# Odd keys moved by SyncE in two parts, key tiles in another order, more unread products, GpSimd pieces of 480 columns

## The chip, the cores and the metric

The kernel runs on one core of a Trainium2 chip. The core has TensorE (matrix products, "PE" in the profile; its weight loads are "PEld"), VectorE ("DVE"), ScalarE ("ACT"), GpSimd ("POOL") and SyncE ("SP"), which here only issues DMAs. Each works through its own list of instructions in order, and semaphores hold an instruction until what it needs is there. The metric is the device time of one execution in microseconds; six executions of the kernel before give a median of 742.34 us (739.19 to 746.28).

## The reference: what is computed

Two branches over the same input x (2048 rows of 512) are mixed by a gate.

```python
q = x @ wq          # 32 heads of 16
k, v = x @ wk, x @ wv        # one key and one value head for all
a = softmax(q k^T / 4) v  @ wo
z = gelu(x @ w_in);  z1, z2 = halves of 688;  z2 = layernorm(z2)
b = (z1 * (w_sp @ z2 + b_sp)) @ w_out
g = sigmoid((x * gate_w).sum(-1));  out = g * a + (1 - g) * b
```

Attention is the bulk: 32 heads times 2048 queries times 2048 keys, so 134 million exponentials.

## The kernel before

**Units and blocks.** A unit is four heads of the same parity with 512 queries; there are 32 units. A unit has 64 blocks: 16 key tiles of 128 keys (kt = 0 to 15) times four groups g of one head each. A block is one score product on TensorE with 32 rows of weights (`s_mm`, recorded on line L313): keys from `KA`, queries from `QA`, 512 columns of PSUM out. `KA` has two planes. In plane 0 the keys stand in rows 32g to 32g+15, and they serve the even units; in plane 1 they stand in rows 32g+16 to 32g+31, for the odd units.

**Two ways to the exponential.** Two blocks at a time (1024 columns) go to ScalarE, whose exponential (`exp_op`, L631) writes them to `P`. Four blocks of one key tile are a batch for VectorE instead: `d_A` (L655) turns 1024 columns of PSUM into a linear term in `X`, twice for each batch, and `d_square` (L667) squares all 2048 columns twice; what comes out approximates the exponential, up to a correction by the products with `MC` and `CC`. Of the second squaring, pieces of `GE` = 416 columns go to GpSimd (`g_piece`, L674): none, one or two for each batch, and VectorE squares the 2048, 1632 or 1216 columns that are left. A piece is made to wait for the VectorE instruction ahead of a `d_A`, so that it runs beside that `d_A`. Products with the values (`ps<-P,V` and `ps<-X,V`) add the blocks up over the keys in one bank; when a unit is complete, VectorE transposes the sum (L685), GpSimd forms the reciprocal and scales (L691, L694, L697), and VectorE transposes back to `OT` (L700).

**The order of keys.** `KL` lists the key tiles. Within a unit ScalarE takes blocks from the front of that list, VectorE's batches from its back.

**Making K.** x arrives in four chunks of 512 rows, transposed by DMA. Chunk c gives key tiles 4c to 4c+3: four products (`k_mm`) and a copy from PSUM to plane 0 by VectorE (`k_ev`, L355). When all four chunks are there, `k_shift` (L359) has GpSimd issue four DMAs of 64 KB that copy plane 0 to plane 1. In `gate_and_k` and `g_MC` the correction is made from the last seven tiles of `KL`; `Kt` (L429) holds two of each chunk's four key tiles, repeated for eight heads.

**The other branch.** SyncE loads x, w_in, b_sp, w_o and w_out, and then `ld_wT(0)` (L302), four transposing loads of w_sp's first quarter, each of which waits for the one before. The products with w_in are spread between the score products; when all of z2 is there, ScalarE does all GELUs in one stretch, and TensorE computes z1 meanwhile. The products with w_sp, w_out and w_o fill the gaps after that.

**What sets the order.** A planner in the kernel's Python code writes the order of every engine's list before the program is built. It keeps a clock for TensorE, ScalarE and VectorE, gives each candidate a ready time, a cost and a priority, and always takes the next for the engine that is free first. Costs are constants: 917 ns for an exponential, 1134 for a `d_A`, `GNS` for a GpSimd piece (a fixed part and a part for each column), with `GLAT` ahead. `T["K1"]` is the time from which it lets odd units be used. Score products for ScalarE come first, and no other TensorE work is placed that would end after the next of them is due. `keep_pick` puts in unread products: it adds up the work of the last 3.4 us, counting a full 512-column product as one, and where the sum is under `KEEP` it offers a product of zeros that nothing reads, or of ones into a free bank; under `LOW` with a better priority.

Of the kernel before, what the change touches and what calls it, by code (L numbers as in the profile page):

```python
# [15 lines left out]
S = 2048  # L16
D = 512
DH = 16
# [13 lines left out]
ZMAX = 25.0  # L32


KL = (0, 1, 2, 4, 5, 8, 9, 12, 13, 6, 10, 14, 15, 11, 7, 3)

NPB = 21
NX = 6
# [2 lines left out]
NMAX = 7  # L41
# [8 lines left out]
DMARG = 50.0  # L50
DRAW = 115.0
RIDE = 0.0
GE = 416
GLAT = 160.0
GNS = (60.0, 2.0)
EMARG = 50.0
EXPT = (0, 491, 917, 1343)
SLATE = 535.0
FREE = 60.0
SEEN = 204.0  # L60
KEEP = 7.5
LOW = 6.5
MMARG = 120.0
PMARG = 200.0
PRE = 12
# [107 lines left out]
def build_kernel(nc, x_d, wq_d, wk_d, wv_d, wo_d, win_d, wsp_d, bsp_d, wout_d, gw_d, out_d):  # L173
    es = ExitStack()
    with es:
# [24 lines left out]
        KA = sb("KA", [128, 2, S], B16)  # L200
        QA = sb("QA", [128, NQ, 512], B16)
        V1 = sb("V1", [128, NKT, 32], B16)
        KT0 = sb("KT0", [128, NKT, DH], B16)
        Kt = sb("Kt", [128, 8, 128], B16)
# [68 lines left out]
        def dma(eng, fn, r=(), w=(), n=16, tag="", after=()):  # L273
            return op(eng, fn, r=r, w=w, dma=n, tag=tag, after=after)
# [23 lines left out]
        def ld_wT(tc):  # L298
            prev = []
            for k in range(4):  # L300
                r0 = 512 * tc + 128 * k
                prev = [dma("sp", lambda q, r0=r0, k=k: q.dma_start_transpose(wT[:, :, 128 * k:128 * k + 128], wsp_d[r0:r0 + 128, :]),  # L302
                            w=[("wT", k)], tag="wT", after=prev)]
        ld_wT(0)

        for g in range(4):
            op("dve", lambda v, g=g: v.tensor_scalar(wk_rep[:, :, 32 * g:32 * g + 16], wk_sb[:], 0.25, None, ALU.mult), r=["wk"], w=["wk_rep"])
# [38 lines left out]
        def setT(k):  # L346
            def f(t):
                T[k] = t
            return f
# [4 lines left out]
        def k_ev(c, b):  # L354
            op("dve", lambda v: v.tensor_copy(KA[:, 0, 512 * c:512 * c + 512], bank(b)), r=[bkey(b)], w=[("K", 0, c)], tag="Kev")  # L355

        def k_shift():
            for g in range(4):
                dma("pool", lambda q, g=g: q.dma_start(KA[32 * g + 16:32 * g + 32, 1, :], KA[32 * g:32 * g + 16, 0, :]),  # L359
                    r=[("K", 0, c) for c in range(4)] + ["KA1"], w=[("K", 1, g)], tag="Ksh")  # L360

        def g_K(c):
            def done(t):
                T[("K", 0, c)] = t
                if c == 3:
                    k_shift()
                    T["K1"] = t + 4500
            return Group("K%d" % c, [(C512, lambda dt=dt: k_mm(c, dt, BM)) for dt in range(4)], [(600, lambda: k_ev(c, BM))],
                         lambda: when(("x", c)), done)

# [46 lines left out]
        def g_V(c):  # L417
            def piece(k, dt):
                t0 = 512 * c + 128 * k
                return lambda: mm(bank(BM, 33, 64 * k), xT[:, dt, t0:t0 + 128], wvg[:, dt, 0:33], dt == 0, dt == 3,  # L420
                                  ["wv", "gw", "wvk", ("x", c)], [BMK], tag="V")
            src = bank(BM, 256).rearrange("p (k w) -> p k w", w=64)
            e1 = lambda: op("dve", lambda v: v.tensor_copy(V1[:, 4 * c:4 * c + 4, 0:DH], src[:, :, 0:DH]), r=[BMK], w=[("V", c)], tag="Vev")
            e2 = lambda: op("dve", lambda v: v.tensor_copy(gs[:, 4 * c:4 * c + 4].unsqueeze(2), src[:, :, 32:33]), r=[BMK], w=[("gs", c)], tag="gsev")
            e3 = lambda: op("dve", lambda v: v.tensor_copy(KT0[:, 4 * c:4 * c + 4, :], src[:, :, 16:32]), r=[BMK], w=[("KT0", c)], tag="ktev")

            def done(t):
                T[("V", c)] = t
                dve_q.append((330, lambda: op("dve", lambda v: v.tensor_copy(  # L429
                    Kt[:, 2 * c:2 * c + 2, :].rearrange("p k (h d) -> p k h d", d=DH),  # L430
                    KT0[:, 4 * c + 2:4 * c + 4, :].unsqueeze(2).broadcast_to([128, 2, 8, DH])), r=[("KT0", c)], w=[("Kt", c)], tag="Kt"), t, setT(("Kt", c))))
                if c == 3:
                    gate_and_k()
            def all_():
                for k in range(4):
                    for dt in range(4):
                        piece(k, dt)()
            return Group("V%d" % c, [(480, all_)], [(150, e1), (100, e2), (130, e3)],
                         lambda: when(("x", c), "wvg"), done)
# [15 lines left out]
        def g_MC():  # L455
            pieces = []
            for h in range(2):
                for i in range(NMAX):
                    kt = KL[15 - i]
                    pieces.append((90, lambda h=h, i=i, kt=kt: mm(  # L460
                        bank(BM, 32 * (NMAX - i), 256 * h + 32 * i).rearrange("p (n e) -> p n e", e=32),
                        Kt[:, 2 * (kt // 4) + kt % 2, :] if h == 0 else ones[:, 0:128], V1[:, kt, :].unsqueeze(1).broadcast_to([128, NMAX - i, 32]),
                        i == 0, i == NMAX - 1, [("Kt", kt // 4), ("V", kt // 4), "ones"], [BMK], tag="MC")))
            msrc = bank(BM, 32 * NMAX).rearrange("p (n e) -> p n e", e=32).unsqueeze(2).broadcast_to([128, NMAX, 8, 32])
            mk = mke[:].unsqueeze(1).unsqueeze(3).broadcast_to([128, NMAX, 8, 32])
            e1 = lambda: op("dve", lambda v: v.tensor_tensor(MC[:], msrc, mk, ALU.mult), r=[BMK, "mke"], w=["MC"], tag="MC")  # L466
            e2 = lambda: op("dve", lambda v: v.tensor_scalar(ct[:, 0, :], bank(BM, 32 * NMAX, 256), E0, None, ALU.mult), r=[BMK], w=["ct0"], tag="CC")
            cc = CC[:, :, :].rearrange("p n e -> p (n e)")
            e3 = lambda: op("dve", lambda v: v.tensor_copy(cc, ct[:, 0, :]), r=["ct0"], w=["CC"], tag="CC")
            e4 = lambda: op("dve", lambda v: v.tensor_tensor(ct[:, 1, :], ct[:, 0, :], cc, ALU.subtract), r=["ct0", "CC"], w=["ct1"], tag="CC")  # L470
            e5 = lambda: op("dve", lambda v: v.tensor_scalar(ct[:, 1, :], ct[:, 1, :], s01[:, 1:2], None, ALU.mult), r=["ct1", "s01"], w=["ct1"], tag="CC")
            e6 = lambda: op("dve", lambda v: v.scalar_tensor_tensor(cc, cc, s01[:, 0:1], ct[:, 1, :], ALU.mult, ALU.add), r=["CC", "ct1", "s01"], w=["CC"], tag="CC")
            def some(h):
                for c_, f_ in pieces[NMAX * h:NMAX * h + NMAX]:
                    f_()
            return Group("MC", [(500, lambda: some(0)), (500, lambda: some(1))], [(1950, e1), (320, e2), (320, e3), (320, e4), (250, e5), (320, e6)],
                         lambda: when(*[(k, c) for k in ("Kt", "V") for c in range(4)]), setT("MC"))
# [140 lines left out]
        def s_mm(b, blk):  # L618
            u, kt, g = blk
            par = u % 2  # L620
            rk = [("K", 0, kt // 4)] if par == 0 else [("K", 1, g)]
            mm(bank(b), KA[32 * g:32 * g + 32, par, 128 * kt:128 * kt + 128], QA[32 * g:32 * g + 32, (u // 2) % NQ, :], True, True,
               rk + [("Q", (u // 2) % NQ)], [bkey(b)], tp=(32 * g, 0), tag="S")

# [870 lines left out]
```

## Time and profile before

| | |
|---|---|
| six runs | 739.19 to 746.28 us, median 742.34 |
| the profiled execution | 739.42 us, its span 737.6 us |
| busy, of the span | PE 94%, DVE 97%, ACT 97%, POOL 41% |
| exponentials on ScalarE | 752, the first at 9.17 us, the last ends at 726.8 us |
| GELU stretch on ScalarE | 164.3 to 189.0 us |
| granted TensorE clock, mean | 0.998 of full speed |

The span is the time from the first to the last instruction of the profiled execution. A group line names the source line, the engine, the operation and the tiles, then how often it ran, its busy time and the mean length of one; the idle time at its end is that of the engine just before these instructions, with what ended it. A record can overlap the next one on the same engine, so the mean length can be more than the step from one to the next. "PEclk" is the granted clock in tenths for 40 slices of the span, where 9 is 90% or more. A timeline line has the start and the length in us, the engine (a "q" marks its issuing part), the line and the operation.

### The profile page before, as it was taken

The numbers are of one execution on the slowest core, as the hardware profiler recorded it, in microseconds if no ns is written. First come the engines' busy times: TensorE is split into PE (matmuls) and PEld (weight loads), VectorE is DVE, ScalarE is ACT, GpSimd is POOL, SyncE is SP. The second block draws the span as 40 slices with busy tenths as digits, with TensorE's granted clock in tenths as the row PEclk, the third lists the DMA queues.
The fourth block names the chain that finished last, engine by engine and source line by source line (L and its number), as shares of the span: only waits on it lengthen the run. The fifth ranks groups of instructions, "written<-read, shape, count | busy, mean of one in ns | idle before, by whom it ended". The sixth has DMA issues, their size and how long they took to land.

```text
span 737.6 us, 14117 instructions
## 1 busy us (share of the span) xinstructions
PE 692.3 (94%) x5529; PEld 191.6 (26%) x5529; DVE 713.2 (97%) x821; ACT 717.8 (97%) x781; POOL 303.0 (41%) x304
## 2 busy tenths in 40 slices
PE   8899989989899999999999999999999999999995
PEld 2322222223222222222222322222222222222221
DVE  7999999999999999999999999999999999999996
ACT  5999999999999999999999999999999999999994
POOL 4245444340444344444344443444554433334440
PEclk9999999999999999999999999999999999999999
DMA  9810000000000001400000140000004000000001
GB/s 202 190 30 1 1 1 1 2 1 0 1 1 1 2 1 30 94 15 8 1 1 1 31 94 16 8 1 1 1 21 96 16 15 1 1 1 1 1 1 33
DMA packets 49115, 17.06 MB, mean 23 GB/s; under 512 B 44146, under 2 KB 48978, under 8 KB 49043
## 3 DMA queue, kind: packets, MB, share of 16 engines
q1 hardware_dynamic: 45986, 15.02, 9.0%
q10 hardware_dynamic: 2928, 0.82, 0.6%
q8 instruction: 45, 0.74, 0.4%
q0 software_dynamic: 128, 0.26, 0.2%
q14 instruction: 28, 0.22, 0.1%
HBM read 3.25 MB, written 2.10 MB: 7 GB/s over the span
## 4 chain that ended last, share of the span: by engine, by line
ACT 58%; PE 19%; issue 18%; DVE 3%; POOL 1%; ACTq 0%; POOLq 0%
ACT P L631 56%; PE ps L313 13%; PE ps L312 6%; DVE X L655 1%; ACT z L521 1%; DVE X L667 1%; ACT z L529 1%; DVE MC L466 0%; POOL bspz L264 0%; POOL KA L261 0%; DVE KA L355 0%; ACTq L161 0%; ACT L631 0%; ACT L529 0%; DVE outsb L1321 0%
## 5 line engine op out<-in xcount | busy, mean ns | idle before, releaser
L631 ACT ACTIVATE P<-ps 128x1024 bf16<-128x1024 f32 x752 | 691.4, 1117 | 3.2 <-PE ps L313 2.7
L313 PE MATMUL ps<-QA,KA 32*128 32x512 bf16 x2048 | 317.5, 384 | 33.6 <-ACT P L631 27.1
L655 DVE TENSOR_SCALAR X<-ps 128x1024 f16<-128x1024 f32 x272 | 329.5, 1212 | 6.8 <-PE ps L313 5.7
L674 POOL TENSOR_TENSOR X<-X 128x416 bf16<-128x416 f16 x189 | 166.1, 879 | 343.7 <-DVE X L667 251.9
L667 DVE TENSOR_TENSOR X<-X 128x2048 f16<-128x2048 f16 (+3 forms) x272 | 290.7, 1074 | 2.0
L313 PEld LDWEIGHTS ps<-QA,KA 32*128 32x128 bf16 x2048 | 78.1, 91 | 319.5 <-ACT P L631 292.9
L313 PE MATMUL ps<-P,V 128*32 128x512 bf16 x1504 | 136.9, 384 | 0.0
L691 POOL TENSOR_TENSOR rc<-T,mone 128x16 f32<-128x16 f32 x31 | 94.7, 3055 | 52.6 <-DVE T L685 52.5
L312 PE MATMUL ps<-wT,z 128*128 128x512 bf16 x320 | 100.4, 385 | 0.0
L313 PE MATMUL ps<-X,V 128*32 128x512 bf16 x544 | 66.5, 385 | 0.2 <-DVE T L685 0.2
L313 PEld LDWEIGHTS ps<-P,V 128*32 128x32 bf16 x1504 | 28.5, 94 | 43.2 <-issue 42.5
L312 PEld LDWEIGHTS ps<-wT,z 128*128 128x128 bf16 x320 | 22.5, 97 | 47.6 <-issue 43.2
L312 PE MATMUL ps<-wout,z 128*128 128x512 bf16 x96 | 29.9, 385 | 0.7 <-DVE sq L613 0.4
L312 PE MATMUL ps<-win,xT 128*128 128x344 bf16 x128 | 29.6, 314 | 0.2
L685 DVE STREAM_TRANSPOSE T<-ps 128x512 f32<-128x512 f32 x32 | 22.7, 710 | 1.7 <-PE ps L313 1.6
L312 PE MATMUL ps<-wo,OT 128*128 128x512 bf16 x64 | 21.4, 385 | 1.6 <-DVE OT L700 1.6
L312 PE MATMUL ps<-ones 128*128 128x512 bf16 x64 | 21.4, 411 | 1.5 <-DVE ones L256 1.5
L697 POOL TENSOR_TENSOR Tn<-T,rcg 128x256 bf16<-128x256 f32 x31 | 21.3, 687 | 2.4
L313 PEld LDWEIGHTS ps<-X,V 128*32 128x32 bf16 x544 | 15.6, 94 | 17.3 <-issue 15.3
L312 PE MATMUL ps<-xT,wq 128*128 128x512 bf16 x64 | 19.9, 384 | 0.0
L312 PE MATMUL ps<-ones,zeros 128*128 128x512 bf16 x54 | 19.4, 386 | 0.0
L312 PE MATMUL ps<-xT,win 128*128 128x512 bf16 x80 | 18.3, 380 | 0.9 <-ACT z L521 0.7
(113 smaller groups left out, 291.3 us busy)
## 6 DMA issues: line engine op xcount, KB each, us to landing
out_dram<-outsb SPq DMA_DIRECT2D x14, 128.0 KB, 1.7
win<-in_B_w_in_dram SPq DMA_DIRECT2D x2, 688.0 KB, 6.5
wout<-in_B_w_out_dram SPq DMA_DIRECT2D x1, 640.0 KB, 8.8
wo<-in_A_wo_dram SPq DMA_DIRECT2D x1, 512.0 KB, 7.5
wq<-in_A_wq_dram ACTq DMA_DIRECT2D x1, 384.0 KB, 8.2
wT<-in_B_w_sp_dram SPq DMA_TRANSPOSE x16, 4.4
KA<-KA POOLq DMA_DIRECT2D x4, 64.0 KB, 2.7
out_dram<-outsb ACTq DMA_DIRECT2D x2, 128.0 KB, 2.9
```

What stands on the lines that cost most here:

```text
L312: return t.matmul(dst, lhsT, rhs, start=start, stop=stop)
L313: return t.matmul(dst, lhsT, rhs, start=start, stop=stop, tile_position=tp)
L521: op("act", lambda a: a.activation(z1[:, 1024 * i:1024 * i + 1024], bank(b, 1024), ACT.Gelu_apprx_tanh), r=[bkey(b), bkey(b + 1)], w=[("z1 ...
L529: op("act", lambda a: a.activation(z, z, ACT.Gelu_apprx_tanh), r=[("z2", st) for st in sts], w=[("z2", st) for st in sts], tag="gelu2")
L631: op("act", lambda a: a.activation(P[:, 512 * p:512 * (p + n)], ps[:, 512 * b0:512 * (b0 + n)], ACT.Exp), r=[bkey(b0 + i) for i in range(n ...
L655: op("dve", lambda v: v.tensor_scalar(X[:, m % NX, 1024 * h:1024 * h + 1024], bank(BD, 1024), PA, PB, ALU.mult, ALU.add), r=[bkey(BD), bke ...
L667: op(eng, lambda v: v.tensor_tensor(x if tag == "dU" else x.bitcast(B16), x, x, ALU.mult), r=ks, w=ks, tag=tag)
L674: op("pool", lambda g: g.tensor_tensor(x.bitcast(B16), x, x, ALU.mult), r=ks, w=ks, after=[pg.ops["dve"][-1]], tag="gW")
L685: o("dve", lambda v: v.transpose(T1[:], bank(BO)), r=[("bk", BO)], w=["T1"], tag="T1")
L691: o("pool", lambda g: g.tensor_tensor(rc[:].unsqueeze(2), lsum, mone[:].unsqueeze(2), ALU.pow), r=["T1", "mone"], w=["rc"], tag="rc")
L697: o(e, lambda v: v.tensor_tensor(tn, t1[:, :, 0:16], s_[:].unsqueeze(2).broadcast_to([128, 16, 16]), ALU.mult), r=["T1", k], w=[("Tn", pr, ...
```

## The change

`KL` has another order: the tiles 6 and 10 move forward, so that the twelve tiles of chunks 0 to 2, all but 3, 7 and 11, come before those of chunk 3. The odd keys are copied by SyncE instead of GpSimd, in two parts: keys 0 to 1535 when the first three chunks are there, the last 512 after the fourth. The first load of w_sp is issued behind them, and no longer straight after the weights. Score products of odd units wait for the part that they read. `Kt` holds all four tiles of chunk 3 and one of each other chunk. `GE` goes from 416 to 480, with other planning costs for GpSimd; `KEEP` and `LOW` go up by 0.5 each.

```diff
-KL = (0, 1, 2, 4, 5, 8, 9, 12, 13, 6, 10, 14, 15, 11, 7, 3)
+KL = (0, 1, 2, 4, 5, 6, 8, 9, 10, 12, 13, 14, 15, 11, 7, 3)
...
-GE = 416
+GE = 480
 GLAT = 160.0
-GNS = (60.0, 2.0)
+GNS = (190.0, 1.65)
...
-KEEP = 7.5
-LOW = 6.5
+KEEP = 8.0
+LOW = 7.0
...
-        ld_wT(0)
...
-        def k_shift():
+        def k_shift(z):
+
+            lo, hi = ((0, 1536), (1536, S))[z]
             for g in range(4):
-                dma("pool", lambda q, g=g: q.dma_start(KA[32 * g + 16:32 * g + 32, 1, :], KA[32 * g:32 * g + 16, 0, :]),
-                    r=[("K", 0, c) for c in range(4)] + ["KA1"], w=[("K", 1, g)], tag="Ksh")
+                dma("sp", lambda q, g=g: q.dma_start(KA[32 * g + 16:32 * g + 32, 1, lo:hi], KA[32 * g:32 * g + 16, 0, lo:hi]),
+                    r=[("K", 0, c) for c in (range(3) if z == 0 else (3,))] + ["KA1"], w=[("K", 1, g, z)], tag="Ksh")
...
+                if c == 2:
+                    k_shift(0)
                 if c == 3:
-                    k_shift()
-                    T["K1"] = t + 4500
+                    k_shift(1)
+                    ld_wT(0)
+                    T["K1"] = t + 5000
...
-                dve_q.append((330, lambda: op("dve", lambda v: v.tensor_copy(
-                    Kt[:, 2 * c:2 * c + 2, :].rearrange("p k (h d) -> p k h d", d=DH),
-                    KT0[:, 4 * c + 2:4 * c + 4, :].unsqueeze(2).broadcast_to([128, 2, 8, DH])), r=[("KT0", c)], w=[("Kt", c)], tag="Kt"), t, setT(("Kt", c))))
+                n, k0 = (1, 4 + c) if c < 3 else (4, 0)
+                dve_q.append((66 + 134 * n, lambda: op("dve", lambda v: v.tensor_copy(
+                    Kt[:, k0:k0 + n, :].rearrange("p k (h d) -> p k h d", d=DH),
+                    KT0[:, 4 * c + 4 - n:4 * c + 4, :].unsqueeze(2).broadcast_to([128, n, 8, DH])), r=[("KT0", c)], w=[("Kt", c)], tag="Kt"), t, setT(("Kt", c))))
...
-                        Kt[:, 2 * (kt // 4) + kt % 2, :] if h == 0 else ones[:, 0:128], V1[:, kt, :].unsqueeze(1).broadcast_to([128, NMAX - i, 32]),
+                        Kt[:, kt - 12 if kt > 11 else 4 + kt // 4, :] if h == 0 else ones[:, 0:128], V1[:, kt, :].unsqueeze(1).broadcast_to([128, NMAX - i, 32]),
...
-            rk = [("K", 0, kt // 4)] if par == 0 else [("K", 1, g)]
+            rk = [("K", 0, kt // 4)] if par == 0 else [("K", 1, g, kt // 12)]
```

In the built program the lists of SyncE and GpSimd differ only by these DMAs and by the size of the pieces. TensorE has 76 unread products of zeros in place of 54 and otherwise the same products; VectorE's second squarings have 1088 (68), 1568 (53) and 2048 columns (15), in place of 1216 (76), 1632 (37) and 2048 (23). The order within the lists differs from near the start to the end, since the planner works with other numbers.

## The prediction

> **What bounds the kernel now.** I read the busy times first, then the forms of the costly groups, then ScalarE's own timeline with its gaps. The columns of a group line are: count, busy us, mean ns of one, then idle time before it and who ended it.
>
> ```profile
> span 737.6 us, 14117 instructions
> PE 692.3 (94%) x5529; PEld 191.6 (26%) x5529; DVE 713.2 (97%) x821; ACT 717.8 (97%) x781; POOL 303.0 (41%) x304
> PEclk9999999999999999999999999999999999999999
> L631 ACT ACTIVATE P<-ps 128x1024 bf16<-128x1024 f32 x752 | 691.4, 1117 | 3.2 <-PE ps L313 2.7
> ```
>
> ScalarE (ACT) and VectorE (DVE) are both at 97%, so the totals alone don't say which sets the end. The exponentials do: 752 of them hold 691.4 us, 0.919 us each, while one record lasts 1117 ns; the records overlap, and the step between their ends is 0.915 to 0.919 us for 9 in 10. I take 0.9165 as what ScalarE can do. 24.7 us more are the GELU stretch (164.3 to 189.0 us), the rest a head of 9.17 us before the first exponential and a tail of 10.8 us after the last. Adding up what each step takes beyond 0.9165 over the whole span gives 5.1 us of waiting. That is all a better order can win while ScalarE has 752 exponentials. The largest part is one place; ScalarE's timeline (start, length, instructions, and in brackets the idle time before):
>
> ```profile
> 12.68 10.43 ACT L631 ACTIVATE P<-ps 128x1024 bf16<-128x1024 f32 x11 [0.58 <-PE ps L313]
> 24.55 3.77 ACT L631 ACTIVATE P<-ps 128x1024 bf16<-128x1024 f32 x4 [1.45 <-PE ps L313]
> 28.29 32.61 ACT L631 ACTIVATE P<-ps 128x1024 bf16<-128x1024 f32 x35
> ```
>
> TensorE (PE) and VectorE at the same place name the cause: the score products at 24.12 sat behind the copy of key chunk 3 out of PSUM.
>
> ```profile
> 22.53 0.81 PE L312 MATMUL ps<-ones,zeros 128*128 128x512 bf16 x3
> 24.12 0.40 PE L313 MATMUL ps<-QA,KA 32*128 32x512 bf16 x4 [0.78 <-DVE KA L355]
> 23.39 0.68 DVE L355 CAST KA<-ps 128x512 bf16<-128x512 f32 x1
> ```
>
> **The change part by part.** The counts of the built programs differ little. ScalarE has the same 752 exponentials and VectorE the same 136 batches of squares, so no exponential moves to the other engine.
>
> *Order of key tiles.* Before, exponential 15 needs tile 12, the first of chunk 3. Now chunk 2 is used up first and tile 12 comes with exponential 19, four steps later: 4 x 0.9165 = 3.7 us, against a wait of 1.45 us. The copy of chunk 3 stands at the same place in VectorE's order, so the wait goes. Gain: 0 to 2.0 us (with the 0.58); I take 1.4. What is late next: tile 12's scores would be issued when exponential 17 ends, near 25.9 us, and the copy ends near 24.4 to 25.1, so nothing within sight.
>
> *Odd keys on SyncE.* Removed: four DMA issues from GpSimd. Added: eight on SyncE. Past them moves the first load of w_sp, four transposes.
>
> ```profile
> 15.10 0.99 SPq L294 DMA_DIRECT2D wout<-in_B_w_out_dram  x1
> 18.15 0.43 SPq L296 DMA_DIRECT2D wout<-in_B_w_out_dram  x1
> 18.62 9.58 SPq L302 DMA_TRANSPOSE wT<-in_B_w_sp_dram  x2
> 24.37 2.15 POOL L359 DMA_DIRECT2D KA<-KA  x4 [1.08 <-DVE KA L355]
> KA<-KA POOLq DMA_DIRECT2D x4, 64.0 KB, 2.7
> wout<-in_B_w_out_dram SPq DMA_DIRECT2D x2, 48.0 KB, 7.1
> ```
>
> SyncE has issued its loads by 18.6 us; chunk 2 was copied out at 17.8. So the first four go out at 18.6 to 20.6 (4 x about 0.5), and if the queue serves in order, they land after the last piece of w_out: 18.15 + 0.43 + 7.1 = 25.7, plus at most 2.7 = 28.4. Their first reader in the new order is the VectorE batch issued before exponential 25, which is near 30 us. Cover: 1.6 us. If it is gone, the score products queue behind that one on TensorE, and each us late costs ScalarE about one. The second four wait for chunk 3 (near 25), land near 29, and are first read by exponential 45, near 49 us. The w_sp transposes, behind both on SyncE, start at 27 and need four times 4.4 to 4.8 us; they are wanted after z2's normalisation, past 189 us. Nothing else stands on SyncE until the outputs. GpSimd loses 2.15 us of issuing, where one squaring beside it took 1.04 instead of 0.92 us (VectorE 0.1). Value: 0, from -0.2 to +2.
>
> *Pieces of 480 columns.* VectorE's last squares, by form:
>
> ```profile
> L674 POOL TENSOR_TENSOR X<-X 128x416 bf16<-128x416 f16 x189 | 166.1, 879 | 343.7 <-DVE X L667 251.9
> L667 DVE TENSOR_TENSOR X<-X 128x1216 bf16<-128x1216 f16 x76 | 59.1, 778 | 0.0
> L667 DVE TENSOR_TENSOR X<-X 128x1632 bf16<-128x1632 f16 x37 | 36.9, 999 | 0.1
> L667 DVE TENSOR_TENSOR X<-X 128x2048 bf16<-128x2048 f16 x23 | 29.8, 1295 | 0.0
> ```
>
> Together 125.8 us. The new counts are 68 of 1088 columns, 53 of 1568 and 15 of 2048; by the slope (999 - 778) / 416 = 0.53 ns a column they take 0.710, 0.965 and 1.295: 48.3 + 51.1 + 19.4 = 118.8. VectorE saves 7 us, and the end gains nothing from it, since VectorE isn't last. GpSimd has 189 pieces as before, each longer. The trace has one size. In proportion 480 columns take 1,014 ns; with a fixed part of 0.1 us, as the memsets have (2048 columns 1.80, 512 columns 0.52 us), 999. I take 1,000, +0.12.
>
> *Here a rule speaks against the change.* A piece runs beside VectorE's read of PSUM (L655). In the trace it ends 177 ns before that instruction does, and the next squaring starts 76 ns before that end: 100 ns of room. The longer piece overruns by about 20. The Trainium skill's page "SBUF — State Buffer", section "Who interferes with whom", says that a VectorE instruction with two SBUF inputs contends with a GpSimd instruction that reads SBUF, that whoever came first holds the shared port for its whole instruction, and that the other is fully blocked. The trace agrees: a 2048-column squaring beside GpSimd's L697 takes up to 1.65 us instead of 1.21. By the row without the rule, this part is -7 us of VectorE time; with it, 137 pieces are followed by a squaring at once, 137 x 0.02 = 2.7 us are given back, and -4 are left. Both ends are off ScalarE's path: 0. The cover is VectorE's own idle time, about 24 us, of which some 13 lie between head and tail.
>
> *Unread products.* 76 in place of 54: 22 x 0.22 us, plus 0.1 for each change of tiling, make 5 to 7 us of TensorE work in 737. TensorE's weight loads wait 292.9 us for exponentials in all (690 waits), and the planner puts such a product only where it ends before the next score product is due. Cost 0; if none were hidden, 7. What can it bring? The page "TensorE: Matmul & The Clock Gate", Part 1, says that an idle window of about 3.4 us halves the clock, and that the window runs free, so its place differs from run to run. The profiled execution shows a granted clock of 1.0 until the last matmul, so in it the gain is nothing. But it took 739.42 us, and the runs shown 739.19 to 746.28. If dips in other runs make that difference, more products remove part of it. By the row: 0; by the rule: up to the 2.9 us between the profiled time and the median. I take half, 1.5; no run here shows it.
>
> *GELU stretch.* There the new order has two more score groups for VectorE (0.32 us each on TensorE) and two separate waves of products with V (0.54) among the z1 products, 1.2 us more. TensorE idles 0.24 + 0.25 + 0.25 us there for ScalarE, and behind it 32 products run without a gap (7.08 us) with ScalarE following. So 0 to 0.5 is added; I take 0.4.
>
> *Tail.* The last waves read exponentials alone, where before one waited for a squaring that ended at 727.1, just after the last exponential (726.8). Six products of w_out instead of five stand ahead. I take -0.3, from -0.5 to +0.3. The copies to Kt (4 of 224 ns, now three shorter and one longer) change nothing.
>
> **Sum.** Against its own time: 739.42 - 1.4 + 0.4 - 0.3 = 738.1. The median of the runs lies 2.9 above the profiled time. 742.34 - 1.3 - 1.5 = **739.5**, 0.4% less. A measurement of this kernel can hardly tell less than 0.5%, 3.7 us, from no change.
>
> **Rivals.**
> *More is gained.* The products hold the clock in every run, so that the median falls to the profiled kind, 742.34 - 1.3 - 2.9 = 738.1, and new order takes 1 us of the 3.5 us of small waits that are left: 737. For it speaks the spread of the runs, against it that a profile with full clock has no dip to remove. Chance 0.36.
> *Slower: the port.* The pieces overrun by more than worked out, and squarings are blocked. VectorE then has 13 + 7 = 20 us to lose; over 137 pieces that is 0.146 us each, and from there VectorE sets the end. At 0.2 us each (beside L697 it is up to 0.44) it is 27 - 20 = 7 more: 749. For it: only 100 ns of room; against it: the piece would have to take 1.12 us or more. Other waits of the new order, or the keys late on SyncE, can add some us as well, but not 3.7 by themselves. Chance 0.19.
> *The change does nothing.* The wait for chunk 3 turns into another and the clock is as before: 742. It is part of the case "the same", as is my forecast; together 0.45.
>
> **How the numbers follow.** Same 0.45 (own range 738.7 to 743), faster 0.36, slower 0.19. The range: below, all 5.1 us of waits cannot go, so 736; above, up to 745.5, which leaves about 0.1 on each side.
>
> **What would show it.** ScalarE's wait near 24 us is gone, and the steps stay at 0.917; GpSimd's pieces take 0.96 to 1.02 us, and squarings after them lengthen by less than 50 ns; VectorE's busy time falls by 4 to 7 us; KA's transfers land before 28.4. Wrong: a wait for KA near 30 us, squarings well above 1.0 us by their size, or a granted clock under 1.

## The result and the profile after

The changed kernel takes 737.84 us in the median of 31 runs (736.64 to 742.32), the kernel before 742.8 us (739.19 to 751.23, 68 runs). The ratio is 0.9936, with a 95% interval from 0.9919 to 0.9952: 0.64% less time, a little more than the 0.5% that a measurement of this kernel can tell from no change. The forecast was 739.5 us. The result lies in the outer range of the prediction (736 to 745.5), but below the 738.7 to 743 that it gave for its own case, and nearest to the rival "more is gained" (737, chance 0.36).

First the page of the changed kernel (busy times, granted clock, two groups, one DMA issue):

```profile
span 735.2 us, 14176 instructions
PE 698.8 (95%) x5551; PEld 194.3 (26%) x5551; DVE 705.8 (96%) x821; ACT 717.5 (98%) x781; POOL 329.9 (45%) x300
PEclk9999999999999999999999999999999999999999
L636 ACT ACTIVATE P<-ps 128x1024 bf16<-128x1024 f32 x752 | 690.9, 1108 | 1.6 <-PE ps L312 1.3
L679 POOL TENSOR_TENSOR X<-X 128x480 bf16<-128x480 f16 x189 | 186.6, 987 | 314.9 <-DVE X L672 209.7
KA<-KA SPq DMA_DIRECT2D x4, 48.0 KB, 6.2
```

ScalarE still has 752 exponentials, and is still the engine that sets the end. The waiting straight before them fell from 3.2 to 1.6 us. TensorE has 6.5 us more work, VectorE 7.4 us less, GpSimd 26.9 us more. ScalarE's timeline shows where the wait went:

```profile
9.31 2.85 ACT L636 ACTIVATE P<-ps 128x1024 bf16<-128x1024 f32 x3 [0.49 <-PE ps L312]
12.98 16.61 ACT L636 ACTIVATE P<-ps 128x1024 bf16<-128x1024 f32 x18 [0.81 <-PE ps L312]
29.38 30.86 ACT L636 ACTIVATE P<-ps 128x1024 bf16<-128x1024 f32 x33
```

Where the kernel before waited 1.45 us at 24.55, the exponentials now run on from 12.98 through 29.6. The 0.81 us at 12.98, behind x chunk 1, which landed at 12.10, is the largest wait that is left.

The profiled execution took 737.02 us, against 739.42 before. The 2.40 us are made up as follows, with every step of an exponential beyond 0.9165 us counted as waiting (with 752 x 0.9165 us each column adds up to its span within 0.2 us; the differences are what counts):

| part of ScalarE's time | before | after | difference |
|---|---|---|---|
| first exponential starts | 9.17 | 9.31 | +0.14 |
| waiting between exponentials, sum | 5.08 | 2.89 | -2.19 |
| GELU stretch | 23.54 | 23.79 | +0.25 |
| after the last exponential | 10.80 | 10.19 | -0.61 |

That is half of the gain. The medians differ by 4.96 us, and 2.4 of these are in the profiles. The rest is in the runs whose clock was not full. Every run has a mean granted TensorE clock, 0.998 where it was full until the last product, and the times follow it: over 95 runs of the kernel before, 0.01 less of clock goes with 5.4 us more (correlation -0.96). The median of the runs at full clock (0.997 and above) is 739.76 us before and 737.19 after; the medians of all lie 3.0 and 0.65 us above these. Under 0.995 were 65% of the runs of before and 18% of the runs of after. From here on every run is counted, also the few that the comparison of the medians leaves out.

So there are two gains of about 2.5 us each to be explained: one at full clock, and one by fewer drops of the clock.

### The profile page after: what moved, and what is told of

Same layout as the page of the kernel before. It is cut to its first block, busy times and chain, and to the rows that moved or that the text cites. A ratio compares the mean times of both kernels' runs of the same rounds, so it can differ in the third digit from the quotient of the medians.

```text
span 735.2 us, 14176 instructions
## 1 busy us (share of the span) xinstructions
PE 698.8 (95%) x5551; PEld 194.3 (26%) x5551; DVE 705.8 (96%) x821; ACT 717.5 (98%) x781; POOL 329.9 (45%) x300
## 4 chain that ended last, share of the span: by engine, by line
ACT 56%; PE 19%; issue 18%; DVE 6%; POOL 1%; ACTq 0%; POOLq 0%
ACT P L636 56%; PE ps L312 11%; PE ps L311 7%; DVE X L660 2%; DVE X L672 1%; DVE z L548 1%; DVE T L690 0%; DVE MC L471 0%; POOL bspz L264 0%; POOL KA L261 0%; ACTq L161 0%; ACT L636 0%; ACT z L526 0%; DVE outsb L1326 0%; DVE OT L705 0%
## 5 line engine op out<-in xcount | busy, mean ns | idle before, releaser
L679 POOL TENSOR_TENSOR X<-X 128x480 bf16<-128x480 f16 x189 | 186.6, 987 | 314.9 <-DVE X L672 209.7
L672 DVE TENSOR_TENSOR X<-X 128x2048 f16<-128x2048 f16 (+3 forms) x272 | 283.8, 1051 | 1.7
L312 PE MATMUL ps<-P,V 128*32 128x512 bf16 x1504 | 138.9, 384 | 0.0
L696 POOL TENSOR_TENSOR rc<-T,mone 128x16 f32<-128x16 f32 x31 | 97.1, 3132 | 48.3 <-DVE T L690 48.3
L312 PE MATMUL ps<-X,V 128*32 128x512 bf16 x544 | 69.7, 385 | 0.2 <-DVE T L690 0.2
L312 PEld LDWEIGHTS ps<-P,V 128*32 128x32 bf16 x1504 | 28.7, 94 | 41.6 <-issue 41.1
L311 PE MATMUL ps<-ones,zeros 128*128 128x512 bf16 x76 | 28.0, 388 | 0.0
L702 POOL TENSOR_TENSOR Tn<-T,rcg 128x256 bf16<-128x256 f32 x31 | 25.8, 833 | 2.4
```

The costliest lines, as they stand in the source:

```text
L311: return t.matmul(dst, lhsT, rhs, start=start, stop=stop)
L312: return t.matmul(dst, lhsT, rhs, start=start, stop=stop, tile_position=tp)
L672: op(eng, lambda v: v.tensor_tensor(x if tag == "dU" else x.bitcast(B16), x, x, ALU.mult), r=ks, w=ks, tag=tag)
L679: op("pool", lambda g: g.tensor_tensor(x.bitcast(B16), x, x, ALU.mult), r=ks, w=ks, after=[pg.ops["dve"][-1]], tag="gW")
L696: o("pool", lambda g: g.tensor_tensor(rc[:].unsqueeze(2), lsum, mone[:].unsqueeze(2), ALU.pow), r=["T1", "mone"], w=["rc"], tag="rc")
L702: o(e, lambda v: v.tensor_tensor(tn, t1[:, :, 0:16], s_[:].unsqueeze(2).broadcast_to([128, 16, 16]), ALU.mult), r=["T1", k], w=[("Tn", pr, ...
```

## The experiments

The theory of the prediction gave the first gain to the order of the key tiles (SyncE and the pieces being worth nothing at the end) and the second to the unread products. The rivals: that the order only exchanges one wait for another; that the pieces or the planner's new numbers bring the gain; that the clock is held by something else than the products; and that longer pieces block VectorE at the port. All runs in one table. "Full" is the median of the runs at a clock of 0.997 or more, with their number, and "dropped" is the number of runs with a mean clock under 0.995. In the row of before, the 95 runs that stood beside the experiments are pooled. The ratio is to the runs of before on the same chip, with its 95% interval.

| kernel | exps | zeros / ones | median us | full (runs) | dropped | ratio |
|---|---|---|---|---|---|---|
| before | 752 | 54 / 64 | 742.96 | 739.76 (27) | 62 of 95 | |
| after | 752 | 76 / 64 | 737.84 | 737.19 (18) | 6 of 33 | 0.9936 [0.9919, 0.9952] |
| e12 after, once more | 752 | 76 / 64 | 737.94 | 737.63 (7) | 1 of 12 | 0.9939 [0.991, 0.9968] |
| e3 before + order | 754 | 52 / 65 | 742.64 | none | 9 of 12 | 0.9978 [0.9942, 1.0013] |
| e5 before + SyncE | 752 | 54 / 64 | 741.06 | 739.97 (3) | 5 of 10 | 0.9988 [0.9946, 1.003] |
| e11 before + order + SyncE | 752 | 50 / 77 | 737.52 | 736.88 (4) | 4 of 10 | 0.992 [0.9886, 0.9954] |
| e1 after, old products | 752 | 44 / 76 | 738.49 | 737.16 (5) | 6 of 12 | 0.9939 [0.9902, 0.9976] |
| e2 before + more products | 754 | 84 / 76 | 745.27 | 740.67 (3) | 7 of 12 | 1.0008 [0.9973, 1.0043] |
| e7 after, still more products | 752 | 137 / 83 | 739.32 | 739.25 (10) | 0 of 12 | 0.9946 [0.9923, 0.9969] |
| e8 after, no such products | 750 | 0 / 12 | 764.06 | none | 4 of 4 | 1.0318 [1.0253, 1.0382] |
| e4 before + 480 columns | 750 | 56 / 60 | 740.69 | 737.10 (1) | 7 of 12 | 0.9952 [0.9914, 0.9991] |
| e9 after, 416 columns | 752 | 68 / 71 | 740.41 | 738.24 (5) | 7 of 12 | 0.9966 [0.9935, 0.9997] |
| e6 after, 544 columns | 752 | 69 / 77 | 737.18 | 737.18 (6) | 0 of 6 | 0.9906 [0.987, 0.9941] |
| e13 the same as e6 | 752 | 69 / 77 | 737.76 | 737.65 (9) | 2 of 12 | 0.9924 [0.9893, 0.9955] |

The ones include 12 at the start, all that e8 keeps. The same kernel differs at full clock from one series of runs to another: by up to 0.5 us in the changed one (after and e12, e6 and e13), by up to 1.1 us in the kernel before (739.50, 740.62 and 739.75, from 6, 6 and 15 runs). Smaller differences say nothing. The planner decides anew with every edit: 750 or 754 exponentials mean one batch more or less for VectorE, and two exponentials are 2 x 0.917 = 1.83 us for ScalarE.

### The order of the keys, and SyncE

**The order alone.**

```diff
-KL = (0, 1, 2, 4, 5, 8, 9, 12, 13, 6, 10, 14, 15, 11, 7, 3)
+KL = (0, 1, 2, 4, 5, 6, 8, 9, 10, 12, 13, 14, 15, 11, 7, 3)
...
+                n, k0 = (1, 4 + c) if c < 3 else (4, 0)
...
-                        Kt[:, 2 * (kt // 4) + kt % 2, :] if h == 0 else ones[:, 0:128],
+                        Kt[:, kt - 12 if kt > 11 else 4 + kt // 4, :] if h == 0 else ones[:, 0:128],
```

> The kernel before with the new order of key tiles alone (and the key copies for the correction that go with it); 754 exponentials. Both theories: the wait of 1.45 us near 24 us is gone. Theory A: 739.4 - 1.5 + 1.8 = 739.7 at full clock, and since the unread products are few (52 and 65), the median lies 3 us above: 742 to 743.5. Rival B: the gain is there without them, so the median is 740 to 741.

The wait for chunk 3 was gone: ScalarE ran from 19.24 to 30.5 without a break. But no run came near 737, and in the profiled execution (745.15 us) the timelines of TensorE, GpSimd's issuing and ScalarE show a longer wait a few us on:

```profile
29.68 0.39 PE L313 MATMUL ps<-QA,KA 32*128 32x512 bf16 x2 [0.19 <-ACT P L632]
31.73 0.60 PE L313 MATMUL ps<-QA,KA 32*128 32x512 bf16 x1 [1.66 <-DMA KA<-KA]
32.90 0.60 PE L313 MATMUL ps<-QA,KA 32*128 32x512 bf16 x1 [0.57 <-DMA KA<-KA]
...
25.07 2.15 POOL L359 DMA_DIRECT2D KA<-KA  x4 [1.28 <-DVE KA L355]
...
35.06 1.02 ACT L632 ACTIVATE P<-ps 128x1024 bf16<-128x1024 f32 x1 [3.50 <-PE ps L313]
```

GpSimd can't issue before chunk 3 is copied out (25.07). Its four transfers took 4.1 us here (median, issue to landing), 2.7 in the kernel before; the last two landed at 31.68 and 32.86 us, where in the kernel before all had landed by 28.95. The first score products that read the odd keys stood in TensorE's list at 30. They waited 1.66 + 0.57 us for the transfer; the clock was half from 31.3 to 41.6 us, and ScalarE lost 3.50 us. In this execution one wait had taken the place of the other, as the rival had it.

That it does so in every run isn't shown. e3 has two exponentials more than before, 1.83 us, and so has e2 below, which keeps the old order and was measured beside it. The two best runs of e3 took 739.50 and 739.79 us at a clock of 0.996; e2 took 742.05 and 742.13 at that clock, and 740.59 to 741.19 at full clock. So in some runs the order alone already gained about 1 us or more. Had the last transfer landed 2.4 us after the end of its issue, as in the kernel before, the keys would have been there at 29.6, in time (an estimate: 27.22 + 2.4). But none of e3's 12 runs had a full clock, and 9 dropped.

**SyncE alone.**

```diff
-        ld_wT(0)
...
-                dma("pool", lambda q, g=g: q.dma_start(KA[32 * g + 16:32 * g + 32, 1, :], KA[32 * g:32 * g + 16, 0, :]),
+                dma("sp", lambda q, g=g: q.dma_start(KA[32 * g + 16:32 * g + 32, 1, lo:hi], KA[32 * g:32 * g + 16, 0, lo:hi]),
...
+                if c == 2:
+                    k_shift(0)
                 if c == 3:
-                    k_shift()
-                    T["K1"] = t + 4500
+                    k_shift(1)
+                    ld_wT(0)
+                    T["K1"] = t + 5000
```

> The kernel before with the odd keys moved by SyncE in two parts and the first load of w_sp behind them, nothing else; 752 exponentials, the same numbers of unread products. The wait of 1.45 us near 24 us stays, since it is for chunk 3 itself. Theory A: at full clock 739.4 as before, within 0.7 us, median as the kernel before within 1.5 us. Rival E (the transfer by SyncE is worth something by itself): best run 738.5 or less.

At full clock it took 739.97 us, as before (739.76), and the wait of 1.44 us for chunk 3 was where it had been.

**Both together**, nothing else.

> The kernel before with the new order of key tiles and with the odd keys moved by SyncE; pieces of 416, KEEP and LOW as before; 752 exponentials, 50 products of zeros and 77 of ones. The order alone ran into a wait of TensorE for the transfer of the odd keys near 31 us, 3.5 us for ScalarE. Theory F (the order only pays with the earlier transfer): no wait for that transfer, none for chunk 3, full clock 737 to 738; the clock dips in half of the runs or more, median 739 to 742. Rival: a wait for the odd keys of over 1 us is left.

736.88 us at full clock, against 739.75 for before and 737.63 for e12, measured beside it on the same chip: 2.9 us, the whole of the gain at full clock. The median, 737.52, is as good as the whole change's. In its profiled execution the clock was half from 13.5 to 23.7 us, but past that ScalarE's timeline runs through both places, that of chunk 3 and that of the odd keys, without a wait:

```profile
23.44 11.27 ACT L636 ACTIVATE P<-ps 128x1024 bf16<-128x1024 f32 x12 [0.50 <-PE ps L312]
34.59 0.22 ACT L448 ACTIVATE eg<-gs 128x16 f32<-128x16 f32 x1
34.70 9.37 ACT L636 ACTIVATE P<-ps 128x1024 bf16<-128x1024 f32 x10
```

So the edit on SyncE, worth nothing alone, takes away the wait that the new order can run into: with it the keys 0 to 1535 leave before chunk 3 is there. The timeline of SyncE in the changed kernel shows it:

```profile
19.00 0.42 SPq L296 DMA_DIRECT2D wout<-in_B_w_out_dram  x1
19.47 7.62 SPq L360 DMA_DIRECT2D KA<-KA  x8
27.13 16.25 SPq L302 DMA_TRANSPOSE wT<-in_B_w_sp_dram  x4
```

The issues begin at 19.47, 5.6 us before GpSimd's 25.07 in e3. That more than pays for the slower landing behind the weights on that queue (6.2 us): the first four had landed at 26.89 us, the second four at 28.36. No profile of a kernel with both edits shows a score product that waits for these transfers. How the 2.9 us divide between the two edits is not settled: less the 1.83 us for its two exponentials, e3's two best runs stand at 737.7 and 738.0, about 1 us above e11 at full clock and 0.3 above e11's two runs at their clock (737.29 and 737.72), and its other runs higher.

### The clock, and the unread products

**The place of chunk 3 drops the clock too.** The profile of e5 caught what the profile of before had not. Its ScalarE timeline from 24.5 us:

```profile
24.55 3.77 ACT L635 ACTIVATE P<-ps 128x1024 bf16<-128x1024 f32 x4 [1.44 <-PE ps L312]
...
30.08 1.02 ACT L635 ACTIVATE P<-ps 128x1024 bf16<-128x1024 f32 x1 [0.49 <-PE ps L312]
31.48 1.02 ACT L635 ACTIVATE P<-ps 128x1024 bf16<-128x1024 f32 x1 [0.38 <-PE ps L312]
33.00 3.24 ACT L635 ACTIVATE P<-ps 128x1024 bf16<-128x1024 f32 x3 [0.50 <-PE ps L312]
```

Busy times in stretches of 3.4 us (stretch, its length, then busy us of PE, PEld, DVE, ACT and POOL with counts, granted clock, DMA share, GB/s), of e5:

```profile
23.50:26.90 3.40, 2.07 (x26) 0.80 (x26) 3.26 (x7) 2.35 (x3) 0.00 (x0) 0.98 0.32 74
26.90:30.30 3.40, 3.04 (x33) 1.19 (x33) 1.69 (x10) 2.77 (x5) 0.66 (x1) 0.50 0.75 156
30.30:33.70 3.40, 3.40 (x28) 1.54 (x26) 1.55 (x2) 2.53 (x3) 0.23 (x1) 0.52 0.13 30
```

The same view of the kernel before (the first stretch, then the one behind it):

```profile
23.50:26.90 3.40, 2.08 (x27) 0.84 (x28) 3.27 (x7) 2.35 (x3) 2.15 (x4) 1.00 0.92 169
26.90:30.30 3.40, 3.35 (x50) 1.44 (x48) 2.13 (x11) 3.40 (x6) 0.65 (x1) 1.00 0.88 195
```

And of the kernel after:

```profile
23.50:26.90 3.40, 3.16 (x37) 1.09 (x35) 3.37 (x6) 3.40 (x5) 0.44 (x1) 1.00 0.33 71
```

Before and e5 have the same thin stretch, in which TensorE works 2.1 of 3.4 us since it waits for chunk 3. In one execution the clock stays, in the other it is half for the next 6.8 us, the score products come late, and ScalarE waits three times more, 1.37 us. In e4, which has the same order, the clock fell at the same place, from 26.8 to 33.6 us.

The traces also show what differs. Within an execution the changes of the clock lie on a grid of 3.413 us: the half-clock stretches of the profiles last 1, 2, 3, 4 or 11 such steps (in e8 also 6, 8 and 10), and e4's two drops, at 26.75 and 187.18 us, lie 47 steps apart. Where the grid lies differs from one execution to the next. In e5 one step holds nearly all of the thin stretch; in the profile of before, counted back from the one change of its clock (at 734.71 us, behind the last products), a border at 24.74 cuts it in two. First the step of e5, then the two of before:

```profile
23.34:26.75 3.41, 1.93 (x27) 0.80 (x26) 3.34 (x8) 2.20 (x3) 0.00 (x0) 1.00 0.36 89
21.33:24.74 3.41, 2.63 (x30) 1.08 (x26) 3.41 (x6) 1.97 (x3) 1.25 (x2) 1.00 1.21 276
24.74:28.15 3.41, 2.71 (x45) 1.11 (x40) 2.67 (x10) 3.41 (x4) 1.78 (x4) 1.00 0.80 150
```

So whether a thin place costs clock depends on where the grid happens to lie. In the changed kernel this stretch is filled (3.16). The wait that the order takes away thus costs twice: once by itself, and again in those executions where the clock falls behind it. How many of the 62 dropped runs of before fell here isn't known, since only a profile shows the place. Of the profiles with the old order, e4 and e5 lost the clock here, e2 and e4 behind the GELU stretch. With the new order, SyncE and some filling products none lost it here, but e9, e11 and e13 lost it at 12 to 14 us, behind the wait for x chunk 1, and e1 and e12 behind the GELU stretch.

**The old number of products in the changed kernel.**

```diff
-KEEP = 8.0
-LOW = 7.0
+KEEP = 7.5
+LOW = 6.5
```

> The kernel after, with KEEP and LOW back at 7.5 and 6.5; still 752 exponentials, 44 products of zeros and 76 of ones instead of 76 and 64. Theory A (order of keys wins about 2.4 us in an undisturbed execution, and the unread products win another 2.5 us because they keep the granted clock up in more executions): an execution at full clock takes 737 to 738 us, but the median goes back to 739.5 to 741 and some runs show a clock of 0.99 or less. Rival B (the whole gain is order, the unread products do nothing): median 737.5 to 738.5, and the clocks are as in the kernel after.

At full clock 737.16 us, so the added products cost nothing there (737.19). The median is 0.65 us above that of after, which the intervals don't tell apart. What differs is the tail of the distribution: 6 of 12 runs had a dropped clock, against 7 of 45 of the changed kernel (after and e12 together), and the worst took 751.61 us. In the mean the runs lie 3.8 us above their full clock, 1.0 in after and 0.2 in e12, and 4.6 in the kernel before measured beside e1; without its two longest runs, e1 is still 2.0 above, with 4 of 10 dropped. The longest was profiled. Its windows behind the GELU stretch (columns as above):

```profile
180.00:190.00 10.00, 8.62 (x45) 1.87 (x45) 8.55 (x15) 8.22 (x10) 5.85 (x3) 0.70 0.00 0
190.00:200.00 10.00, 9.39 (x48) 1.55 (x47) 6.89 (x15) 7.78 (x9) 2.63 (x3) 0.50 0.01 2
200.00:210.00 10.00, 9.52 (x47) 1.69 (x48) 6.31 (x7) 6.90 (x7) 4.19 (x4) 0.50 0.00 0
```

The same view of the kernel after:

```profile
180.00:190.00 10.00, 7.60 (x62) 2.47 (x56) 9.54 (x20) 9.79 (x11) 4.56 (x2) 1.00 0.01 2
190.00:200.00 10.00, 9.37 (x66) 2.47 (x62) 10.00 (x20) 10.00 (x12) 6.20 (x6) 1.00 0.00 1
```

At half clock TensorE is as busy as ever (9.4 of 10 us), but it gets 48 products done in the time of 66, and ScalarE works 7 to 8 us of 10 instead of 10. This lasted from 183.9 to 221.5 us. The 3.4 us ahead of it were thin again, 2.07 us of work: ScalarE changes its table there (1.28 us), and no score product is due. The changed kernel has that thin place too (2.01 us from 183.1 to 186.5), and in the profile of e12 the clock fell there, for 3.4 us.

**More products on the kernel before.** (`KEEP` 8.0, `LOW` 7.0)

> The kernel before with KEEP and LOW at 8.0 and 7.0 alone; the planner then gives ScalarE 754 exponentials instead of 752, which is 2 x 0.917 = 1.8 us more. Theory A: at full clock about 741.3 us, median within 1 us of that (742), so the distance of median to best run falls from 3.4 to about 1. Rival B: the distance stays at 3 us or more, median 744 to 745.

No gain: 745.27 us, and 7 of 12 runs dropped, about as often as before. At full clock (3 runs) it took 740.67 us, against 739.50 for before beside it: 1.2 us more, where two more exponentials would account for 1.83. The products alone don't hold the clock of the old order.

**None, and still more, in the changed kernel.** (`KEEP` and `LOW` 0.0; then 9.0 and 8.0)

> The kernel after with KEEP and LOW at zero: no unread products after the twelve at the start; 750 exponentials, 1.8 us less than 752. Theory A: the clock drops in every run and stays down for long; mean clock under 0.97, 750 us or more. Rival B (unread products do nothing for the time): 735 to 736.5.

> The kernel after with KEEP and LOW at 9.0 and 8.0: 137 products of zeros and 83 of ones instead of 76 and 64, still 752 exponentials. Theory A (unread products hold the clock, and at full clock they cost nothing): all runs at a clock of 0.996 or more, best run 736.5 to 737.5 as in the kernel after, median within 0.5 us of the best, so about 737.3. Rival D (80 more products of 0.22 us, 18 us of TensorE work, delay score products): best run 738.5 or more.

Without the filling products every run dropped, and the median is 764.06. The page of e8:

```profile
span 758.8 us, 13850 instructions
PEclk8899999998599999999999999998589999965697
```

With 137 products of zeros not one run of 12 dropped, but at full clock they cost 739.25 - 737.18 = 2.1 us (against e6, measured beside it; 1.6 against e12): the first exponential starts at 10.07, the waits sum to 3.46, the tail is 11.3. Such products are free only where TensorE has time left; the setting of the change lies between a cost in every run and a cost in some.

Put together, by the number of dropped runs: old order or GpSimd's transfers, 83 of 129 with the old number of products and 7 of 12 with the new one (e2); the new order with SyncE, 10 of 22 with the old number and 16 of 75 with the new. Of these steps the products in the new order are the surer one (10 of 22 against 16 of 75, and all and none at the ends, e8 and e7). That the order and SyncE alone make drops rarer (83 of 129 against 10 of 22) could still be chance, about one in ten by an exact test: by the mean over the runs, e11 lies 1.4 us above its full clock, against 3.2 for before beside it, but e1 with its 3.8 is hardly better than before with 4.6. What the products bring shows only together with the new order (e2). It isn't clean: e9 belongs to the last group and dropped in 7 of 12, and what in its plan does that stays open. In its profile the clock fell at 12.3 us, behind the wait for x chunk 1, where the changed kernel is thin as well.

### Pieces of 480 columns

**In the kernel before**, `GE` 480 and the new `GNS`:

> The kernel before with pieces of 480 columns and the new planning costs of GpSimd alone; 750 exponentials and 137 batches of squares, so VectorE takes one batch more. Theory A: 739.4 - 1.8 = 737.6 at full clock with the wait near 24 us as before, median about 740 to 741.5. Rival C (the pieces block VectorE's squarings): squarings after a piece are 50 ns or more longer than by their columns, and the time is 742 or more.

**In the changed kernel**, back to 416 and the old `GNS`:

> The kernel after with pieces of 416 columns and the old planning costs of GpSimd; 752 exponentials as in the kernel after, 68 products of zeros and 71 of ones. Theory A: VectorE's saving by the longer pieces is idle time, so the best run is 737.2 within 0.7 us, and VectorE's busy time rises by about 7 us. Rival C (the longer pieces bring a part of the gain): best run 738.5 or more.

The first came out at 0.9952 of before, but its planner gave ScalarE only 750 exponentials: a gift of 1.83 us that the whole change doesn't have. Back to 416, with 752 exponentials as in the changed kernel, VectorE is busy 711.6 us instead of 705.8, and at full clock the time is 738.24, against 737.18 for 544 columns beside it. This is 1.1 us for the larger pieces (five runs at 416, 737.34 to 739.20); yet e11 has 416 columns as well and reaches 736.9. So the saved time of VectorE doesn't bring it. What is left is the order that the planner finds with each size, about 1 us either way; no run separates that.

**544 columns**, run twice, to make the port show itself:

> The kernel after with pieces of 544 columns; 752 exponentials. By the two sizes seen (879 and 987 ns) a piece takes 1,095 ns and ends about 40 ns after the PSUM read beside it, so 120 ns after the next squaring starts. If the shared port is locked: a squaring right after a piece takes 0.1 us or more longer than its columns say, VectorE gives back 10 us or more, and the time rises to 738 to 742. Rival (squarings and pieces don't hold each other up): squarings of 960 and 1504 columns take 0.65 and 0.93 us, time as the kernel after, 737.2 at full clock.

> The kernel after with pieces of 544 columns, again, with more runs. If it beats the kernel after: median at least 0.5 us below it, best run not higher, and a clock of 0.996 or more in nearly all runs. If the six runs before were luck: the same dips as in the kernel after, medians within 0.5 us.

The forms of the squarings in the kernel after (mean ns second behind the bar), then in e6:

```profile
L672 DVE TENSOR_TENSOR X<-X 128x1568 bf16<-128x1568 f16 x53 | 51.4, 969 | 0.2
L672 DVE TENSOR_TENSOR X<-X 128x1088 bf16<-128x1088 f16 x68 | 48.9, 720 | 0.0
L672 DVE TENSOR_TENSOR X<-X 128x2048 bf16<-128x2048 f16 x15 | 18.5, 1232 | 0.0
```

```profile
L679 POOL TENSOR_TENSOR X<-X 128x544 bf16<-128x544 f16 x189 | 206.8, 1094 | 300.1 <-DVE X L672 198.7 <-DVE z L517 31.7 <-DVE z L574 23.5
L672 DVE TENSOR_TENSOR X<-X 128x960 bf16<-128x960 f16 x71 | 45.9, 646 | 0.0
L672 DVE TENSOR_TENSOR X<-X 128x1504 bf16<-128x1504 f16 x47 | 44.1, 941 | 0.2
```

At 480 columns a piece takes 987 ns and overlaps the next squaring by about 10 ns; the squarings take 720 and 969 ns, against 710 and 965 by their columns. At 544 a piece takes 1,094 ns and ends some 120 ns after the next squaring has started. By the slope of 0.53 ns a column from the forms of after, the squarings should take 652 and 935; they take 646 and 941. So the rival "slower: the port" didn't come true: an overlap of this length costs nothing.

The port does block, though, where a squaring starts earlier beside a piece. Two places in the timelines of the kernel after, each time the piece and then the squaring:

```profile
412.99 0.99 POOL L679 TENSOR_TENSOR X<-X 128x480 bf16<-128x480 f16 x1
413.76 0.80 DVE L672 TENSOR_TENSOR X<-X 128x1088 bf16<-128x1088 f16 x1
455.65 0.99 POOL L679 TENSOR_TENSOR X<-X 128x480 bf16<-128x480 f16 x1
456.09 1.63 DVE L672 TENSOR_TENSOR X<-X 128x2048 f16<-128x2048 f16 x1
```

The first squaring starts 0.22 us before the end of its piece and takes 0.09 us longer than the median of its form (0.71); the second starts 0.55 us before that end and takes 0.42 us longer (1.63 in place of 1.21). The traces hold 12 such cases (after, e2, e6, e7, e8, e11, e12 and e13), with 0.22 to 0.93 us of the piece left: each squaring took longer by what was left of the piece less 0.13 us. That agrees with the rule of the Trainium skill's page "SBUF — State Buffer", section "Who interferes with whom", by which a VectorE instruction with two SBUF inputs contends with a GpSimd instruction that reads SBUF, and the shared port is an exclusive lock; only the last 0.13 us of a piece held nothing. (That the other side "fully blocks" stands there beside the 2-port modes, another kind of VectorE instruction; for a squaring it is these cases that show it.) So the room was not 100 ns but about 230 (an estimate: 100 + 130), and pieces of 544 columns, 215 ns longer than those of 416, just fit. In the kernel after three squarings were blocked, for 0.93 us together.

The two series with 544 columns (18 runs, 737.18 and 737.76) are not shown to beat the change, and neither is any other version here.

**The change once more, unedited**, beside e5, e11 and e13:

> The kernel after, unchanged, beside the one with longer pieces on one chip: median 737.5 to 738.5, a clock under 0.995 in about one run of five.

737.94 us, 0.9939: the result of the change again.

## Why the prediction was right, and where it was not

The sum against the profiled execution was 738.1, and it took 737.02; the median was given as 739.5, and is 737.84. The direction holds, and the mechanism of the first gain. Two steps don't hold as they were given, and one came out for another reason.

- **What bounds the kernel.** Held: 752 exponentials, 0.9165 us each, with 5.1 us of waits as the most that could be won; 2.2 of them were.
- **Order of key tiles.** 1.4 us taken, range up to 2.0; the waits fell by 2.19. The size was a little low, since smaller waits went with it. "Nothing within sight" of what is late next was wrong for the order by itself: the odd keys were, in the profiled execution of e3 (3.50 us). It was right for the change as a whole.
- **Odd keys on SyncE.** Zero, and zero it is alone (e5). What the prediction didn't see is that the new order can run into a wait for the keys without it; how much of the 2.9 us at full clock that is worth, the runs don't settle. The cover held: the first four landed at 26.9 us, taken at 28.4 at most, and no score product waited.
- **Pieces.** 1,000 ns taken, 987 measured; VectorE 7 us less by the row, 4 by the rule of the port, 7.4 measured. The row came out, but not because the rule is wrong: a squaring is blocked by a piece (for 0.42 us at 456 us in the kernel after). The step that was mis-sized is the room, 100 ns in the prediction and about 230 by the traces, so that the overlap of 10 ns gave nothing back. The end moves by about 1 us with the planner, in either direction, which the step's 0 left out.
- **Unread products.** 5 to 7 us of TensorE work: 6.5. Cost 0: held (e1). The gain is the step that was off, in size and in what it was put down to. "If dips in other runs make that difference, more products remove part of it" was right on the dips, and 2.4 of 3.0 us went, not 1.5. But on the old order the products remove nothing (e2), and in the new one they lower the mean over the runs by 2.8 us (e1 against after; 1.0 without the two longest runs of e1) and the median by only 0.65. So the clock gain belongs to the order, SyncE and the products together: the order takes away one place where TensorE had too little to do, the products fill others. How much falls to each isn't settled. The rule of the Trainium skill's page "TensorE: Matmul & The Clock Gate", Part 1, that the window runs free and so differs from run to run, agrees with the grid in e5 and before, where the same stretch lost the clock and kept it. That an idle window is needed does not: in the grid step ahead of each drop before the tail in the profiles of e1, e2, e3, e4, e5, e9, e11, e12 and e13, TensorE was busy for 1.6 to 2.3 us of 3.4.
- **GELU stretch** +0.4, measured +0.25. **Tail** -0.3, measured -0.61, a little outside its range. **Kt copies** 0: the first takes 0.19 us in place of 0.23, at 11.90 in both timelines of VectorE.

The 1.1 us that the profile's sum was too high are 0.8 of the order, 0.3 of the tail and 0.15 of the GELU stretch, less 0.14 of the head. The rest of the error in the median is clock, 2.4 in place of 1.5, less 0.46 by which the median of before came out higher with more runs. "The change does nothing" fell with e11; "more is gained" was nearest, with its clock term nearly whole, though the products are only a part of its cause.

Open: which of the 22 added products hold the clock (no run moved single products), how the gains divide between order, SyncE and products, and whether e1 loses the clock behind the GELU stretch more often than after, where the place is as thin; one profile of each can't say.

## What to carry to other kernels

Look for the places where the matrix engine waits before counting its idle time: one wait can cost its own length and, in the runs where the clock's grid lies badly, a stretch at half clock behind it, so compare medians of runs by their granted clock and not only two profiles. When an order is changed to hide one arrival, list the arrivals that the new order needs earlier; an edit that is worth nothing alone may be the one that keeps another from running into them. Filler work for the clock has a setting: none cost 26 us here, nearly twice as many as in the change cost 2 us in every run.

## What the runs showed of the hardware

- The clock falls without an idle window. In the kernels with filling products, TensorE was 47 to 67% busy in the grid step of 3.413 us ahead of each drop before the tail; a step with 66% (after, 182.4 to 185.8 us) kept it. No sharp threshold of busy time comes out: in e8 a step with 83% (28.8 to 32.2 us) lost it.
- The half-clock stretches lasted 3.41, 6.83, 10.24, 13.65 and 37.55 us, multiples of one length. TensorE being 94% busy at half clock (e1, most of its products with 32 rows or columns) didn't bring it back for 37.6 us.
- A squaring of VectorE that starts beside a GpSimd piece took longer by what was left of the piece less 0.13 us (12 cases, 0.22 to 0.93 us left); one that starts 0.12 us before the end (e6) took no longer.
- Four transfers of 48 KB within SBUF took 6.2 us to land on SyncE's queue behind the last weights (6.3 in e5, 4.1 in e11), four of 16 KB 2.0 us after these; four of 64 KB on GpSimd's queue took 2.7 us (before) and 4.1 us (e3).
